# A fused attention and two-layer kernel: block-diagonal q prepared in DRAM, and the padding cleared elsewhere

## The chip, the cores and the metric

The kernel runs on one core of a Trainium2 chip. A core has TensorE (PE) for matrix products, VectorE (DVE) and ScalarE (ACT) for work on elements, GpSimd (POOL), and SyncE (SP), whose queue issues the transfers between DRAM and the on-chip memory. The metric is the device time of one execution in microseconds, median of the runs.

## The reference

Three stages in float32. Attention has 4 batches of 8 heads with 576 positions of 64 numbers; a position sees its own block of 64 positions and all blocks before it. The two layers that follow work on 2304 rows of 512.

```python
scores = scale * np.matmul(q, k.transpose(0, 1, 3, 2))
scores = np.where(block_i >= block_j, scores, -1e9)
attn = np.exp(scores - max);  attn = attn / (sum + 1e-09)
x = (attn @ v).transpose(0, 2, 1, 3).reshape(B * S, H * D)
x = np.maximum(np.maximum(x @ w1, x @ w2), x @ w3) @ w_out      # first layer, d_ff 768
h = x @ w_in;  out = (h * np.cos(h)) @ w_out2                   # second layer, d_ff 2048
```

## The kernel before

**Items.** Attention is cut into 32 items: 4 batches, two halves of the positions (320, then 256), four pairs of heads. The two heads of a pair share the 128 partitions, 64 each. For one block of 64 positions, q of the pair is laid out as a 128x128 block-diagonal tile: head 0 in the upper left quarter, head 1 in the lower right, zeros elsewhere. One product of it with k gives the scores of both heads. An item of the first half has 5 such blocks (640 columns), of the second 4 (512).

**Precision.** From item 4 on, q and k are split into a rounded high part and a rest (`kh`, `kl`; `qbd` holds two tiles, high and low), and the scores take three fast products. The first four items (`NATIVE`, L547) multiply in plain float32 with no split. For them the scale of the scores is applied in the exponential, so that each row maximum (`top`) is multiplied by it first (`scaled`).

**Zeros before.** The layout is made on the chip: tiles are cleared once (`qnat` for the first items, `qbd` by a cast of zeros), and each item then writes the two diagonal quarters, from partitions 0 to 63 and 64 to 127, so there are two loads (first items) or two scalings and two differences (others), the loop over `a` in `load` (L565) and `prep` (L590). The tiles of probabilities (`prob`) are cleared as well, since an odd block leaves its last 64 columns unwritten, which the transposes read.

**An item's path.** `load`, `prep`, `scores` (L606: products into the PSUM tiles SA and SB, row maximum on VectorE, exponential with a sum on ScalarE, reciprocal, scaling of the probabilities), `transposes` (L648, PSUM tile tb, copied to `pt`), `pv` (L660, PSUM tile X). The output of items 0 to 3 goes straight into `xhi` and `xlo`, the first layer's input for the first 320 rows; later outputs go to DRAM (`x`) and come back as chunks of 512 rows (`load_x`, L688).

**Weights.** `convert` (L506) turns a 512 KB tile of weights, which comes as pairs of 32-bit words (`raw`), into float32 and splits it: on ScalarE two scalings (`t`, `add`), on VectorE a shift of `t`, an `or` with the sign, an integer addition (CUSTOM_DVE_ANT_0 in the trace, ISA in the order), then a cast `whi` on either engine and a difference `wlo`. The first layer has 18 tiles w and 6 tiles wout.

**Order.** Every call is recorded first. A planner (`forward`, L292, with `backward` for ranks) lays the operations out over five engines by estimated costs, chooses an engine where `choose` offers several, and the instructions are then issued in that order. A tile with a `tag` and `bufs` has so many copies in rotation: the next user waits until all operations on the copy's last user are done. Products of the first layer and conversions fill the gaps between the items.

Of the kernel before, what the change touches and what calls it, by code (L numbers as in the profile page):

```python
# [8 lines left out]
F32 = mybir.dt.float32  # L9
F32R = mybir.dt.float32r  # L10
# [3 lines left out]
AF = mybir.ActivationFunctionType  # L14
ALU = mybir.AluOpType
# [4 lines left out]
P = 128  # L20
NLOW, NHIGH = 320, 256
# [4 lines left out]
def f32(ap):  # L26
    return ap.bitcast(F32)
# [414 lines left out]

def fused_kernel(tc, qk, v2, w1, w2, w3, wout, w_in2, w_out2, out):
    B, HP, _, S = qk.shape
    S //= 2
    D = P // 2
    NFF = w1.shape[0]
    NFC = w_in2.shape[0]
# [4 lines left out]
    scale = 1.0 / math.sqrt(D)  # L453

    R = Plan(tc)
    const = R.open(name="const", bufs=1)
    cv = R.open(name="cv", bufs=1)
    moe = R.open(name="moe", bufs=1)
    cv_start = R.open(name="cv_start", bufs=1)
# [3 lines left out]
    at = R.open(name="at", bufs=1, side="right")  # L463
    ps_x = R.open(name="ps_x", bufs=1, space=PSUM, side="right")

    qnat = [cv_start.tile([P, 5, P], F32, f"qnat{i}") for i in range(2)]
    for t in qnat:
        R.vector.memset(t, 0.0)
    ident = const.tile([P, P], F32, "ident")
    R.gpsimd.memset(ident, 0.0)  # L470
    R.gpsimd.affine_select(out=ident, in_=ident, compare_op=ALU.not_equal, fill=1.0, base=0, pattern=[[-1, P]],
                           channel_multiplier=1)
    halfpi = const.tile([P, 56], F32, "halfpi")[:, :1]
    R.gpsimd.memset(halfpi, math.pi / 2)
    NROT = 3
    top = [[const.tile([P, 1], F32, f"top{i}_{j}") for j in range(5)] for i in range(NROT)]
    scaled = [[const.tile([P, 1], F32, f"scaled{i}_{j}") for j in range(5)] for i in range(NROT)]
    sums = [const.tile([P, 5], F32, f"sums{i}") for i in range(NROT)]

    whi = [[moe.tile([P, NK, P], F32R, f"whi{j}_{m}") for m in range(3)] for j in range(NFF)]  # L480
# [53 lines left out]
    for u in range(2):  # L534
        f = Half()
# [13 lines left out]
    items = []  # L549
    for b in range(B):  # L550
        for half in range(2):
            for pair in range(HP):
                it = Item()
# [2 lines left out]
                items.append(it)  # L556

    prob = [at.tile([P, (b // 2 + 1) * P], F32, f"prob{b}") for b in range(S // 64)]
    for b in reversed(range(S // 64)):
        R.vector.memset(prob[b], 0.0)  # L560
    qbd = [at.tile([P, 5, P], F32R, f"qbd{i}") for i in range(2)]
    for t in qbd:
        R.copy(t.rearrange("p b n -> p (b n)"), prob[S // 64 - 1])

    def load(it):  # L565
        f, src = it.f, qk[it.b, it.pair]
        it.raw = at.tile([P, S + NHIGH], F32, "qk", tag="qk", bufs=2)
        q0 = S if it.half else 0
        if it.native:
            it.q = qnat[it.n % 2]  # L570
            q0 = NLOW + S if it.half else 0
            for a in (0, 64):
                R.sync.dma_start(it.q[a:a + 64, 0:len(f.blocks), a:a + 64],
                                 src[a:a + 64, q0:q0 + f.n].rearrange("p (b n) -> p b n", n=64))
            it.k = it.raw[:, 0:f.nk]
            if it.n == 0:
                conv_next()
            R.sync.dma_start(it.k, src[:, NLOW:NLOW + f.nk])
            if it.n == 0:
                conv_next()  # L580
        elif it.half:
            R.sync.dma_start(it.raw, src[:, NLOW:])
            it.k, it.q = it.raw[:, 0:S], it.raw[:, S:]
        else:
            R.sync.dma_start(it.raw[:, 0:2 * NLOW], src[:, 0:2 * NLOW])
            it.q, it.k = it.raw[:, 0:NLOW], it.raw[:, NLOW:2 * NLOW]
        it.vr = at.tile([P, 5, 2, 64], F32, "vr", tag="vr", bufs=2)
        R.sync.dma_start(it.vr[:, 0:f.nj].rearrange("p j a d -> p j (a d)"), v2[it.b, it.pair, :, 0:f.nj])

    def prep(it):  # L590
        f = it.f
        if it.native:
            return
        nb, nk = len(f.blocks), f.nk
        kh = it.kh = at.tile([P, S], F32R, "kh", tag="kh")[:, :nk]
        kl = it.kl = at.tile([P, S], F32R, "kl", tag="kl")[:, :nk]
        R.copy(kh, it.k)
        R.sub(kl, it.k, f32(kh))
        for a in (0, 64):
            q = it.q[a:a + 64].rearrange("p (b n) -> p b n", n=64)  # L600
            hi, lo = (t[a:a + 64, 0:nb, a:a + 64] for t in qbd)
            R.scale(hi, q, scale)
            R.vector.scalar_tensor_tensor(lo, q, scale, f32(hi), ALU.mult, ALU.subtract)


    def scores(it):  # L606

        f = it.f
        sm = sums[it.n % NROT]
        nb = len(f.blocks)  # L610
        for banks, parts in f.tiles:
            if banks == 2:
                s = ps_x.tile([P, 2, 512], F32, "SA", tag="SA", bufs=1)
            else:
                s = ps_x.tile([P, 1, 512], F32, "SB" if parts[0][0] % 2 == 0 or it.half else "SA", tag="SB" if banks == 1 else "SA", bufs=1)
            for bank in range(s.dims[0][1] if banks == 2 else 1):
                with R.unit():
                    first = True
                    for b, c0, n, c in parts:
                        ks = slice(bank * n, bank * n + n)  # L620
                        i = b - f.first
                        prods = [(it.q[:, i], it.k[:, ks])] if it.native else [
                            (qbd[0][:, i], it.kh[:, ks]), (qbd[0][:, i], it.kl[:, ks]), (qbd[1][:, i], it.kh[:, ks])]
                        for x, (q, k) in enumerate(prods):
                            R.tensor.matmul(s[:, bank, c0:c0 + n], q, k, start=first, stop=x == len(prods) - 1,
                                            skip_group_check=True)
                            first = False
            for b, c0, n, c in parts:
                i = b - f.first
                part = s[:, :, c0:c0 + n] if c == 2 else s[:, 0, c0:c0 + n]  # L630
                bias = top[it.n % NROT][i]
                R.vector.tensor_reduce(bias, part, axis=AX.XY if c == 2 else AX.X, op=ALU.max, negate=True)
                if it.native:
                    bias = scaled[it.n % NROT][i]
                    R.vector.tensor_scalar(bias, top[it.n % NROT][i], scale, None, ALU.mult)
                p = prob[b][:, 0:n * c]
                if c == 2:
                    p = p.rearrange("p (c n) -> p c n", c=2)
                R.scalar.activation(p, part, AF.Exp, bias=bias, scale=scale if it.native else 1.0,
                                    accum_out=sm[:, i:i + 1])  # L640
        R.vector.tensor_scalar(sm[:, 0:nb], sm[:, 0:nb], 1e-9, None, ALU.add)
        R.vector.reciprocal(sm[:, 0:nb], sm[:, 0:nb])
        for b in f.blocks:
            i = b - f.first
            p = prob[b][:, 0:64 * (b + 1)]
            R.scale_rows(p, p, sm[:, i:i + 1])
# [105 lines left out]
    def conv_w(n, pool, bufs):  # L752
        if n < 3 * NFF:
            j, m = divmod(n, 3)
            convert((w1, w2, w3)[m][j], whi[j][m].rearrange("p k e -> p (k e)"),
                    wlo[j][m].rearrange("p k e -> p (k e)"), pool, bufs)
        else:
            j = n - 3 * NFF
            convert(wout[:, j], vhi[j], vlo[j], pool, bufs)
# [21 lines left out]
    def conv_next():  # L781
        n = converted[0]
        if n < 4 * NFF:
            if n % 3 < 2 and not wk:
                conv_w(n, cv_start, 4)
            else:
                conv_w(n, cv, CVR)
            converted[0] += 1
# [15 lines left out]
        R.tensor.matmul(warm[:, 0:P], ident, ident, start=True, stop=True)  # L804
    for n in range(LA):
        load(items[n])
    for n in range(NI + 1):
        conv = CONV.get(n, (0, 0, 0))
        if n:
            transposes(items[n - 1])  # L810
        for step in range(3):
            if step == 1 and n < NI:
                scores(items[n])
                if n + LA < NI:
                    load(items[n + LA])
            if step == 2 and n:
                it = items[n - 1]
                pv(it)
                if it.n == HP - 1:
                    R.close(cv_start)  # L820
                    wk = R.open(cv_start, name="wk", bufs=1)
                done = S * it.b + (S if it.half else NLOW) if it.pair == HP - 1 else 0
                while begun[0] < len(parts) and sum(parts[begun[0]]) <= done:
                    fill += zip([*range(1, 3 * NFF + 1)] + NK * [4 * NFF], moe1_units(begun[0]))
                    begun[0] += 1
            for _ in range(conv[step]):
                conv_next()
            units((0.3, 0.35, 0.35)[step])
        if n + 1 < NI:
            prep(items[n + 1])  # L830
        if n > 9 and n % 3:
            ahead()
# [166 lines left out]
```

## Time and profile before

| | us |
|---|---|
| median of 3 runs (902.95 to 903.24) | 902.98 |
| the profiled execution, its own time | 905.14 |
| its span | 903.3 |

| engine | busy us | share of the span |
|---|---|---|
| PE | 878.9 | 97% |
| PE's weight loads | 739.9 | 82% |
| DVE | 553.7 | 61% |
| ACT | 464.1 | 51% |
| POOL | 0.7 | 0% |

A busy time counts an instruction from its start to its end. Matmuls overlap, and their ends are modelled, so a busy PE may still be slow. The granted clock of PE is a share of its full speed. The share over the whole span hides that the stages differ: attention and conversions come first, the second layer, which is nearly all matmuls, fills the second half.

### The profile page before, as it was taken

What the parts mean: (1) busy time and instruction counts of PE and PEld (TensorE: products, weight loads), DVE (VectorE), ACT (ScalarE), POOL (GpSimd) and SP (SyncE); (2) the same over time, 40 slices, a digit from 0 to 9 for tenths busy, and PEclk for the clock granted to TensorE, in tenths of its full rate; (3) what the DMA queues carried; (4) which work ended last, traced back from release to release, by engine and by line L of the source; (5) the groups of instructions that cost most, each with busy time, mean ns of one, the idle gap of its engine ahead of it and who ended that gap; (6) DMA issues with size and microseconds to landing.
All of it is one profiled execution on the core that took longest, in us unless ns stands there. A gap on an engine that the chain in (4) does not pass through costs nothing.

```text
span 903.3 us, 12655 instructions
## 1 busy us (share of the span) xinstructions
PE 878.9 (97%) x4716; PEld 739.9 (82%) x4716; DVE 553.7 (61%) x1112; ACT 464.1 (51%) x1012; POOL 0.7 (0%) x7
## 2 busy tenths in 40 slices
PE   5789998999999999999999999999999999999998
PEld 4579997888888888888899888888888888888897
DVE  7899997544784457433294499555555545454554
ACT  6899988567874677544353434332233223322333
POOL 0000000000000000000000000000000000000000
PEclk8799999999999999999999999999999999999999
DMA  7545476412661227300352571020001000100000
GB/s 224 182 165 181 147 220 226 155 50 80 216 220 43 65 88 238 97 21 19 134 169 94 228 267 59 8 86 1 1 25 46 1 1 1 47 0 1 18 30 24
DMA packets 42781, 87.59 MB, mean 97 GB/s; under 512 B 7648, under 2 KB 20960, under 8 KB 42720
## 3 DMA queue, kind: packets, MB, share of 16 engines
q1 hardware_dynamic: 42720, 86.79, 29.0%
q8 instruction: 37, 0.61, 0.3%
q14 instruction: 24, 0.20, 0.1%
HBM read 65.93 MB, written 20.84 MB: 96 GB/s over the span
## 4 chain that ended last, share of the span: by engine, by line
PE 91%; ACT 3%; DVE 3%; DMA 2%; issue 1%; SPq 0%; ACTq 0%; DVEq 0%
PE psm L207 53%; PE po L207 22%; PE X L207 5%; PE tb L207 4%; PE SA L207 4%; PE SB L207 3%; ACT prob L207 2%; DMA qnat<-qk 1%; DVE t L207 1%; DMA x<-xs 1%; DMA t<-x 1%; DVE top L207 1%; SPq L207 0%; ACT add L207 0%; ACT t L207 0%
## 5 line engine op out<-in xcount | busy, mean ns | idle before, releaser
L207 PE MATMUL psm<-yh,w_in 128*128 128x512 f32 (+1 forms) x640 | 193.4, 368 | 0.0
L207 PE MATMUL po<-w_out,gh 128*128 128x512 f32 x576 | 177.8, 390 | 0.0
L207 ACT ACTIVATE th<-th,halfpi 128x512 f32<-128x512 f32 (+1 forms) x80 | 54.6, 682 | 190.7 <-DVE th L207 190.7
L207 PE MATMUL psm<-xhi,whi 128*128 128x512 f32 (+2 forms) x360 | 137.3, 381 | 3.2 <-ACT xhi L207 2.2
L207 PE MATMUL psm<-xlo,whi 128*128 128x512 f32 (+2 forms) x360 | 133.5, 371 | 1.3 <-DVE xlo L207 1.2
L207 PEld LDWEIGHTS psm<-yh,w_in 128*128 128x128 f32 x640 | 117.1, 188 | 20.7
L207 PE MATMUL psm<-xhi,wlo 128*128 128x512 f32 (+2 forms) x360 | 133.3, 370 | 0.0
L207 PEld LDWEIGHTS po<-w_out,gh 128*128 128x128 f32 x576 | 107.1, 188 | 21.4
L207 PE MATMUL psm<-yl,w_in 128*128 128x512 f32 (+1 forms) x320 | 117.7, 368 | 0.0
L207 PE MATMUL po<-w_out,gl 128*128 128x512 f32 x288 | 112.0, 389 | 0.0
L207 DVE TENSOR_SCALAR th<-psm 128x512 int32<-128x512 f32 (+1 forms) x80 | 51.0, 638 | 78.6 <-PE psm L207 78.6
L207 DVE TENSOR_TENSOR th<-psm,th 128x512 f32<-128x512 f32 (+1 forms) x80 | 51.0, 638 | 54.9 <-ACT th L207 54.9
L207 PEld LDWEIGHTS psm<-xhi,whi 128*128 128x128 f32 x360 | 68.1, 189 | 13.5 <-ACT xhi L207 2.7
L207 PEld LDWEIGHTS psm<-xlo,whi 128*128 128x128 f32 x360 | 68.0, 189 | 10.9 <-DVE xlo L207 2.5
L207 PEld LDWEIGHTS psm<-xhi,wlo 128*128 128x128 f32 x360 | 67.8, 188 | 9.9
L207 DVE TENSOR_TENSOR gl<-th,gh 128x512 fp32r<-128x512 f32 (+1 forms) x80 | 51.0, 637 | 39.8 <-ACT gh L207 39.6
L207 DVE TENSOR_TENSOR hm<-psm,hm 128x512 f32<-128x512 f32 (+2 forms) x60 | 38.1, 636 | 60.3 <-PE psm L207 59.8
L207 ACT CAST gh<-th 128x512 fp32r<-128x512 f32 (+1 forms) x78 | 45.0, 577 | 54.9 <-DVE th L207 54.8
L207 PEld LDWEIGHTS psm<-yl,w_in 128*128 128x128 f32 x320 | 60.3, 188 | 10.6
L207 ACT COPY pt<-tb 128x512 f32<-128x512 f32 (+1 forms) x98 | 53.6, 563 | 23.9 <-PE tb L207 23.5
L207 PEld LDWEIGHTS po<-w_out,gl 128*128 128x128 f32 x288 | 54.0, 188 | 11.4
L207 PE MATMUL tb<-ident,prob 128*128 128x128 f32 x400 | 58.6, 276 | 2.5 <-ACT pt L207 1.0
(99 smaller groups left out, 1346.9 us busy)
## 6 DMA issues: line engine op xcount, KB each, us to landing
raw<-w SPq DMA_DIRECT2D x18, 512.0 KB, 4.1
raw<-w_in SPq DMA_DIRECT2D x16, 512.0 KB, 3.8
raw<-w_out SPq DMA_DIRECT2D x16, 512.0 KB, 3.8
qk<-qk SPq DMA_DIRECT2D x16, 416.0 KB, 3.8
vr<-v SPq DMA_DIRECT2D x16, 320.0 KB, 3.9
kept_in<-both SPq DMA_DIRECT2D x10, 512.0 KB, 3.5
w_in<-kept_in SPq DMA_DIRECT2D x10, 512.0 KB, 9.2
out<-osb SPq DMA_DIRECT2D x18, 256.0 KB, 2.0
```

Of the source, the lines that this page charges most:

```text
L207: return lambda: getattr(real, method)(*[value(a) for a in args], **{k: value(a) for k, a in kw.items()})
```

## The change

q is laid out block-diagonal, zeros included, in DRAM by the host's arrangement of the input, so q has twice as many bytes (640 columns an item in the first half, 512 in the second). An item loads it in one transfer into one tile and treats it in one scaling and, from item 4 on, one difference over 128 partitions. The clears of `qnat` and the casts into `qbd` go. k and q now have separate transfers and tiles; for the first items there are two copies of each, for the others one of each, where one tile `qk` in two copies held both. For the first four items k is multiplied by the scale in place before the scores, and `scaled` goes. Of the `prob` tiles only the 64 padding columns of the five that have them are cleared, on GpSimd. The tile that holds `halfpi` is wider and otherwise unchanged.

```diff
-    qnat = [cv_start.tile([P, 5, P], F32, f"qnat{i}") for i in range(2)]
-    for t in qnat:
-        R.vector.memset(t, 0.0)
...
-    for b in reversed(range(S // 64)):
-        R.vector.memset(prob[b], 0.0)
-    qbd = [at.tile([P, 5, P], F32R, f"qbd{i}") for i in range(2)]
-    for t in qbd:
-        R.copy(t.rearrange("p b n -> p (b n)"), prob[S // 64 - 1])
+    for b in range(0, S // 64, 2):
+        R.gpsimd.memset(prob[b][:, 64 * (b + 1):], 0.0)
 
     def load(it):
         f, src = it.f, qk[it.b, it.pair]
-        it.raw = at.tile([P, S + NHIGH], F32, "qk", tag="qk", bufs=2)
...
+        nq = len(f.blocks) * P
         if it.native:
...
+            it.q = cv_start.tile([P, 5 * P], F32, "qnat", tag="qnat", bufs=2)
+            it.k = cv_start.tile([P, NLOW], F32, "knat", tag="knat", bufs=2)
         else:
...
+            it.q = at.tile([P, 5 * P], F32, "q", tag="q")[:, :nq]
+            it.k = at.tile([P, S], F32, "k", tag="k")[:, :f.nk]
+        q0 = 2 * NLOW + S if it.half else 0
+        R.sync.dma_start(it.q, src[:, q0:q0 + nq])
+        R.sync.dma_start(it.k, src[:, 2 * NLOW:2 * NLOW + f.nk])
...
     def prep(it):
         f = it.f
         if it.native:
+            R.scale(it.k, it.k, scale)
             return
...
-        for a in (0, 64):
-            q = it.q[a:a + 64].rearrange("p (b n) -> p b n", n=64)
-            hi, lo = (t[a:a + 64, 0:nb, a:a + 64] for t in qbd)
-            R.scale(hi, q, scale)
-            R.vector.scalar_tensor_tensor(lo, q, scale, f32(hi), ALU.mult, ALU.subtract)
+        it.qh, it.ql = (at.tile([P, 5 * P], F32R, n, tag=n)[:, :len(f.blocks) * P] for n in ("qh", "ql"))
+        R.scale(it.qh, it.q, scale)
+        R.vector.scalar_tensor_tensor(it.ql, it.q, scale, f32(it.qh), ALU.mult, ALU.subtract)
...
-                if it.native:
-                    bias = scaled[it.n % NROT][i]
-                    R.vector.tensor_scalar(bias, top[it.n % NROT][i], scale, None, ALU.mult)
...
+    prep(items[0])
```

The planner orders all engines anew. On SP, the head of the queue before (`qnat_83` is item 0's q, loaded in halves, `raw` a tile of weights, `qk` a k):

```order
L207 DMA qk<-qk 128x320
L207 DMA raw<-w 128x1024
L207 DMA qnat_83<-qk 64x5x64
L207 DMA qnat_91<-qk 64x5x64
L207 DMA raw<-w 128x1024 x3
L207 DMA qk<-qk 128x320
L207 DMA raw<-w 128x1024
L207 DMA qnat_83<-qk 64x5x64
L207 DMA qnat_91<-qk 64x5x64
L207 DMA vr<-v 128x384 x2
```

and now (`knat` and `qnat` are k and q of the first four items; `k` and `q` of 576 and 512 columns are item 4's):

```order
L207 DMA knat<-qk 128x320
L207 DMA qnat<-qk 128x640
L207 DMA knat<-qk 128x320
L207 DMA raw<-w 128x1024
L207 DMA qnat<-qk 128x640
L207 DMA raw<-w 128x1024
L207 DMA k<-qk 128x576
L207 DMA q<-qk 128x512
L207 DMA vr<-v 128x384
L207 DMA raw<-w 128x1024 x2
```

Item 0's q moved from the third and the eighth line to the second, the first weights from the second to the fourth, and item 4's k and q came into the first ten.

On VectorE, the last conversions before the first row maximum of item 0, and what follows, before:

```order
L207 TENSOR_SCALAR t<-t 128x512
L207 ISA t<-t,add 128x1024
L207 SCALAR_TENSOR_TENSOR t<-raw,t 128x512
L207 TENSOR_SCALAR t<-t 128x512
L207 ISA t<-t,add 128x1024
L207 SCALAR_TENSOR_TENSOR t<-raw,t 128x512
L207 TENSOR_TENSOR wlo_1_192<-t,whi_1_183 128x512
L207 ISA t<-t,add 128x1024
L207 TENSOR_REDUCE top_4_210<-SB 128x1
L207 TENSOR_REDUCE top_2_212<-SB 128x1
L207 TENSOR_SCALAR scaled_4_216<-top_4_210 128x1
```

and now, from VectorE's first instruction:

```order
L207 TENSOR_REDUCE top_4_138<-SB 128x1
L207 TENSOR_REDUCE top_2_142<-SB 128x1
L207 TENSOR_REDUCE top_3_149<-SA 128x1
L207 TENSOR_REDUCE top_1_155<-SA 128x1
L207 TENSOR_REDUCE top_0_160<-SA 128x1
L207 TENSOR_SCALAR t<-t 128x512
L207 SCALAR_TENSOR_TENSOR t<-raw,t 128x512
L207 ISA t<-t,add 128x1024
L207 TENSOR_REDUCE top_4_183<-SB 128x1
L207 TENSOR_REDUCE top_2_187<-SB 128x1
L207 TENSOR_SCALAR add<-raw 128x512
```

The clears (eleven, at the head before) and the first four conversions no longer stand ahead of the first maximum, and `scaled` is gone.

On SP again, the loads of the later items, before (`qk` of 832 columns holds k and q of an item of the second half, `vr` is v, `x_0` the output of item 4):

```order
L207 DMA raw<-w 128x1024 x2
L207 DMA vr<-v 128x640
L207 DMA raw<-w 128x1024
L207 DMA vr<-v 128x640
L207 DMA qk<-qk 128x832
L207 DMA raw<-w 128x1024 x3
L207 DMA vr<-v 128x640
L207 DMA x_0_856<-xs 128x256
L207 DMA qk<-qk 128x640
L207 DMA raw<-w 128x1024
```

and now, for the same stretch:

```order
L207 DMA raw<-w 128x1024 x2
L207 DMA vr<-v 128x640
L207 DMA k<-qk 128x576
L207 DMA raw<-w 128x1024
L207 DMA q<-qk 128x512
L207 DMA raw<-w 128x1024 x3
L207 DMA vr<-v 128x640
L207 DMA x_0_784<-xs 128x256
L207 DMA k<-qk 128x576
L207 DMA q<-qk 128x512
L207 DMA raw<-w 128x1024 x3
L207 DMA q<-qk 128x640
```

The k and the q of an item are two lines, with weights between them, and each waits for the item before to have read the one tile there is.

On PE, 8 of the 16 warm-up matmuls on `ident` stand ahead of item 0's scores now, where all 16 did.

## Rows read from the trace of the kernel before

**Rows 1.** Busy time of each engine by stage, granted clock, DMA (columns: first line).
```profile
core 0: us, PE busy (x) PEld busy (x) DVE busy (x) ACT busy (x) POOL busy (x), PEclk, DMA share, GB/s
14.30:18.00 3.70, 3.65 (x10) 2.90 (x10) 1.86 (x7) 2.76 (x7) 0.00 (x0) 0.50 0.65 234
18.00:57.20 39.20, 29.93 (x157) 20.53 (x157) 35.95 (x106) 34.12 (x99) 0.00 (x0) 0.86 0.51 166
57.20:98.50 41.30, 40.86 (x307) 37.90 (x307) 40.61 (x88) 38.37 (x84) 0.00 (x0) 1.00 0.53 172
98.50:139.00 40.50, 40.50 (x318) 37.42 (x319) 38.50 (x100) 36.63 (x103) 0.00 (x0) 1.00 0.63 196
139.00:152.00 13.00, 11.04 (x72) 8.56 (x70) 10.02 (x20) 9.55 (x20) 0.00 (x0) 1.00 0.75 240
517.00:903.30 386.30, 382.71 (x1778) 320.23 (x1776) 221.55 (x368) 122.26 (x202) 0.00 (x0) 1.00 0.11 39
```

**Rows 2.** Start in order of time: start us, us, engine, operation, out<-in, [idle before].
```profile
0.74 0.39 SPq L207 DMA_DIRECT2D qk<-qk  x1
...
1.18 0.42 SPq L207 DMA_DIRECT2D raw<-w  x1
...
1.36 5.53 PE L207 MATMUL psm<-ident 128*128 128x128 f32 x32 [1.36 <-POOL ident L207]
...
2.23 3.37 DVE L207 MEMSET prob<- 128x384 f32 x9
...
4.15 1.35 ACT L207 CAST qbd<-prob 128x640 fp32r<-128x640 f32 x2 [1.92 <-DVE prob L207]
...
5.41 0.67 ACT L207 ACTIVATE t<-raw 128x512 f32<-128x512 f32 x1
...
6.11 0.43 DVE L207 TENSOR_SCALAR t<-t 128x512 int32<-128x512 int32 x1 [0.51 <-ACT t L207]
...
14.31 2.05 PE L207 MATMUL SB<-qk,qnat 128*128 128x320 f32 x4 [7.43 <-DMA qnat<-qk]
...
16.40 0.76 DVE L207 TENSOR_REDUCE top<-SB 128x1 f32<-128x320 f32 x2 [1.18 <-PE SB L207]
...
18.32 1.24 PE L207 MATMUL SB<-qk,qnat 128*128 128x320 f32 x4 [0.36 <-ACT prob L207]
```

**Rows 3.** Chain that ended last, first 20 us: start us, us, what.
```profile
6.27 7.80 DMA qnat<-qk
```

**Rows 4.** Order of time at 55 to 58 us: fourth xlo, and first layer's dense stretch.
```profile
55.15 0.48 DVE L207 TENSOR_TENSOR xlo<-X,xhi 128x320 fp32r<-128x320 f32 x1
...
57.17 0.42 PE L207 MATMUL psm<-xhi,whi 128*128 128x320 f32 x1 [0.49 <-ACT hm L207]
```

**Rows 5.** Groups by shape: count | busy us, mean ns of one | idle before.
```profile
L207 DVE SCALAR_TENSOR_TENSOR t<-raw,t 128x512 int32<-128x512 int32 x56 | 38.1, 686 | 0.4
...
L207 ACT ACTIVATE t<-raw 128x512 f32<-128x512 f32 x51 | 34.2, 670 | 8.3 <-DMA raw<-w 2.2 <-DVE yl L207 2.1 <-DVE w_out L207 2.0
...
L207 DVE CUSTOM_DVE_ANT_0 t<-t,add 128x1024 uint16<-128x1024 uint16 x38 | 26.0, 685 | 2.7 <-ACT add L207 1.6
...
L207 DVE TENSOR_SCALAR t<-t 128x512 int32<-128x512 int32 x56 | 23.4, 421 | 13.0 <-ACT t L207 12.8
...
L207 DVE SCALAR_TENSOR_TENSOR qbd<-qk,qbd 64x256 fp32r<-64x256 f32 x32 | 13.3, 415 | 0.7 <-ACT qbd L207 0.2
...
L207 DVE TENSOR_TENSOR wlo<-t,whi 128x512 fp32r<-128x512 f32 x18 | 12.2, 684 | 0.0
...
L207 ACT ACTIVATE qbd<-qk 64x256 fp32r<-64x256 f32 x20 | 8.3, 415 | 4.5 <-PE SB L207 4.2
...
L207 ACT CAST kh<-qk 128x320 fp32r<-128x320 f32 x11 | 5.0, 450 | 0.0
...
L207 DVE TENSOR_SCALAR scaled<-top 128x1 f32<-128x1 f32 x20 | 2.7, 143 | 0.0
```

**Rows 6.** DMA issues: count, KB each, median us to landing.
```profile
qk<-qk SPq DMA_DIRECT2D x12, 320.0 KB, 2.9
...
qk<-qk SPq DMA_DIRECT2D x4, 160.0 KB, 2.7
```

More of the change, by code (lines that the diff above doesn't have):

```diff
@@ L444, in fused_kernel @@
     B, HP, _, S = qk.shape
-    S //= 2
+    S //= 3
     D = P // 2
@@ L472, in fused_kernel @@
                            channel_multiplier=1)
-    halfpi = const.tile([P, 56], F32, "halfpi")[:, :1]
+    halfpi = const.tile([P, 176], F32, "halfpi")[:, :1]
     R.gpsimd.memset(halfpi, math.pi / 2)
@@ L476, in fused_kernel @@
     top = [[const.tile([P, 1], F32, f"top{i}_{j}") for j in range(5)] for i in range(NROT)]
-    scaled = [[const.tile([P, 1], F32, f"scaled{i}_{j}") for j in range(5)] for i in range(NROT)]
     sums = [const.tile([P, 5], F32, f"sums{i}") for i in range(NROT)]
@@ L558, in fused_kernel @@
     prob = [at.tile([P, (b // 2 + 1) * P], F32, f"prob{b}") for b in range(S // 64)]
-    for b in reversed(range(S // 64)):
-        R.vector.memset(prob[b], 0.0)
-    qbd = [at.tile([P, 5, P], F32R, f"qbd{i}") for i in range(2)]
-    for t in qbd:
-        R.copy(t.rearrange("p b n -> p (b n)"), prob[S // 64 - 1])
+    for b in range(0, S // 64, 2):
+        R.gpsimd.memset(prob[b][:, 64 * (b + 1):], 0.0)
     def load(it):
         f, src = it.f, qk[it.b, it.pair]
-        it.raw = at.tile([P, S + NHIGH], F32, "qk", tag="qk", bufs=2)
-        q0 = S if it.half else 0
+        nq = len(f.blocks) * P
         if it.native:
-            it.q = qnat[it.n % 2]
-            q0 = NLOW + S if it.half else 0
-            for a in (0, 64):
[L573 to L583, printed above, removed]
-        else:
-            R.sync.dma_start(it.raw[:, 0:2 * NLOW], src[:, 0:2 * NLOW])
-            it.q, it.k = it.raw[:, 0:NLOW], it.raw[:, NLOW:2 * NLOW]
+            it.q = cv_start.tile([P, 5 * P], F32, "qnat", tag="qnat", bufs=2)
+            it.k = cv_start.tile([P, NLOW], F32, "knat", tag="knat", bufs=2)
+        else:
+            it.q = at.tile([P, 5 * P], F32, "q", tag="q")[:, :nq]
[3 more added lines that the diff above has]
+        R.sync.dma_start(it.k, src[:, 2 * NLOW:2 * NLOW + f.nk])
+        if it.n == 0:
+            conv_next()
         it.vr = at.tile([P, 5, 2, 64], F32, "vr", tag="vr", bufs=2)
@@ L592, in prep @@
         if it.native:
+            R.scale(it.k, it.k, scale)
             return
[L594 to L599, printed above, removed]
-            q = it.q[a:a + 64].rearrange("p (b n) -> p b n", n=64)
-            hi, lo = (t[a:a + 64, 0:nb, a:a + 64] for t in qbd)
-            R.scale(hi, q, scale)
-            R.vector.scalar_tensor_tensor(lo, q, scale, f32(hi), ALU.mult, ALU.subtract)
+        it.kh, it.kl = (at.tile([P, S], F32R, n, tag=n)[:, :f.nk] for n in ("kh", "kl"))
+        R.copy(it.kh, it.k)
+        R.sub(it.kl, it.k, f32(it.kh))
+        it.qh, it.ql = (at.tile([P, 5 * P], F32R, n, tag=n)[:, :len(f.blocks) * P] for n in ("qh", "ql"))
+        R.scale(it.qh, it.q, scale)
+        R.vector.scalar_tensor_tensor(it.ql, it.q, scale, f32(it.qh), ALU.mult, ALU.subtract)
     def scores(it):
@@ L621, in scores @@
                         i = b - f.first
-                        prods = [(it.q[:, i], it.k[:, ks])] if it.native else [
-                            (qbd[0][:, i], it.kh[:, ks]), (qbd[0][:, i], it.kl[:, ks]), (qbd[1][:, i], it.kh[:, ks])]
+                        qs = slice(i * P, i * P + P)
+                        prods = [(it.q[:, qs], it.k[:, ks])] if it.native else [
+                            (it.qh[:, qs], it.kh[:, ks]), (it.qh[:, qs], it.kl[:, ks]), (it.ql[:, qs], it.kh[:, ks])]
                         for x, (q, k) in enumerate(prods):
@@ L638, in scores @@
                     p = p.rearrange("p (c n) -> p c n", c=2)
-                R.scalar.activation(p, part, AF.Exp, bias=bias, scale=scale if it.native else 1.0,
+                R.scalar.activation(p, part, AF.Exp, bias=bias, scale=1.0,
                                     accum_out=sm[:, i:i + 1])
@@ L980 @@
     v2 = v2.reshape(B, H // 2, 2, (S + D) // P, P, D).transpose(0, 1, 4, 3, 2, 5)
+    heads = qT.reshape(B, H // 2, 2, D, S // D, D)
+    qd = np.zeros((B, H // 2, 2, D, S // D, 2, D), q.dtype)
+    for e in range(2):
+        qd[:, :, e, :, :, e] = heads[:, :, e]
+    qd = qd.reshape(B, H // 2, P, 2 * S)
+    kT = kT.reshape(B, H // 2, P, S)
     arrays = {
-        "qk": np.concatenate([qT[..., :NLOW], kT, qT[..., NLOW:]], axis=3).reshape(B, H // 2, P, 2 * S),
+        "qk": np.concatenate([qd[..., :2 * NLOW], kT, qd[..., 2 * NLOW:]], axis=3),
         "v2": np.ascontiguousarray(v2.reshape(B, H // 2, P, (S + D) // P, 2 * D)),
```

## Prediction

> **What bounds the kernel now.** I read four views in turn: busy time by stage, the start in order of time, the chain that ended last, and groups of instructions by shape.
>
> The stages [rows 1] show three regimes. From 57.2 us PE is busy for 40.86 of 41.30 us, then 40.50 of 40.50, and its last stage (386.3 us, the second layer) has almost nothing idle. Up to 139 us VectorE is full as well (40.61 of 41.30, 38.50 of 40.50) and ScalarE nearly (38.37, 36.63). Before 57.2 us PE has little to do: its busy time there is made of few, slow matmuls at a granted clock of 0.50 and 0.86. From 139 to 152 us PE idles 1.96 us: the fill of the first rows is used up, and attention rows come back late through DRAM. So time is won only where PE starves, in the first 57 us and a little at 145; what the change does after 152 us is worth nothing unless it makes PE wait.
>
> The start [rows 2]: the first score matmul starts at 14.31 us after 7.43 us of idle PE, waiting for the second half of q. The chain [rows 3] says why: that half is issued at 6.27 us, behind five 512 KB weight loads, and takes 7.80 us. Meanwhile VectorE clears 11 tiles, ScalarE casts two of zeros, and both convert weights from 5.41 and 6.11 us on. The fourth item's xlo, which the first layer's groups need whole, ends at 55.63 us, and the dense stretch of PE starts at 57.17 [rows 4].
>
> **Start.** Removed: 11 clears and two casts of zeros. They lie beside the first loads; useful work could not start before the first weights came at 5.41 us, so they count for nothing (without that cover they would cost VectorE 4.6 us and ScalarE 1.35). What moves is the queue: the new order issues k and the whole q of item 0 first, before any weights. k (160 KB) is issued at 0.74 us; such loads take 2.7 us [rows 6], so it lands at 3.4, and the scaling in place, 128x320 on ScalarE, costs 0.45 (the nearest row, a cast of that shape [rows 5]): 3.9. q (320 KB) goes second, where weights went at 1.18 us [rows 2]; at 2.9 us [rows 6] it lands at 4.1. Its upper end: those 512 KB were read at 5.41. Half of the 16 warm-up matmuls stand ahead of the scores: half of 5.53 us from 1.36 [rows 2] ends at 4.1, and `ident` now waits behind three small clears on GpSimd, which the trace lacks: between nothing and 1.1 us, three times the mean clear on VectorE (3.37 us for 9 larger ones [rows 2]); I take 0.4, since they are 64 columns wide. First scores at 4.6 us (4.1 to 5.6), 9.7 earlier. The first row maximum follows 2.09 us behind (16.40 − 14.31): 6.7 us.
>
> **From there to the fourth xlo** took 55.63 − 16.40 = 39.2 us. I count VectorE's rows of that stretch in both orders. Out: 20 rescalings of the maximum at 0.143 = −2.9 us. In: two more shifts (0.421), one more or (0.686), one more add (0.685) and one fewer wlo (0.684): +1.5; five more casts of weights, which ScalarE loses (VectorE's price bounded by the shift, 0.421): +2.1; and small changes in the scaling of probabilities and copies of transposes, bounded by ±1. Sum near zero. On ScalarE two scalings of k (0.9), two more weight scalings (1.3) and one more for the low words (0.7) stand against those five casts (0.45 or more each): between −1 and +1. So about 39 us again: fourth xlo at 45.9, dense PE at about 47.5, a lead of 9.7 us on PE.
>
> **What the lead is worth.** It is borrowed. Before, 11 weight tiles are converted ahead of the fourth xlo, now 8. Three conversions come later, each 0.421 + 0.686 + 0.685 + 0.684 = 2.48 us on VectorE and 2 × 0.670 on ScalarE: 7.4 and 4.0 us, casts aside. They fall into the stretch where both engines are full already [rows 1], and PE's next work, the scores of items 4 to 11 and what hangs on them, comes from these engines. Left of 9.7: 2.3 on VectorE, 5.7 on ScalarE; VectorE decides.
>
> Then the preparation of q: per item two scalings and two differences on 64 partitions become one of each with twice the columns. VectorE: two differences of 64x256 at 0.415 against one of 512 columns, 0.686 by the `or` of the same form: −0.14 us; ScalarE: two scalings at 0.415 against 0.670: −0.16 [rows 5]. Items 5 to 11: −1.0 and −1.1 us. 3.3 us so far. Last, VectorE has 2.98 us and ScalarE 3.45 us idle between 139 and 152 [rows 1], partly for want of PE; a PE that is ahead gives some of it back: 0 to 3, I take 0.8. Together −4.1 us by the time the second chunk of rows enters PE; behind it PE is dense and its work unchanged (same matmuls, same shapes), so that stays to the end.
>
> The extra zeros in q cost DMA, not compute: 160 KB more per item; at 240 GB/s, the highest rate of these stages, 0.7 us of a load, in stages where the engines of the DMA are 53 to 75% busy [rows 1]. Hidden, as long as the loads are early enough (second rival).
>
> The execution profiled has 905.14 us, its span 903.3. The sum is made against it: 905.1 − 4.1 = 901.0; the median of the runs, 902.98, lies 2.2 below: 898.9. I forecast 899.0, its own range 896.5 to 901 (items' stretch 39.2 ± 2, the last term 0 to 3).
>
> **Rivals.**
> *The lead stays whole.* Weight conversions have slack: the new order shifts them because they are not due. If attention alone feeds PE, 9.7 us arrive: 902.98 − 9.7 = 893.3, or up to 896. For it: a group of the first layer needs its own weight tile alone, and eight are there when the dense stretch begins. Against it: VectorE's 98% in the 41 us that follow [rows 1]; what is put off must be fitted in there.
>
> *Loads too late.* Before, the tile that holds q and k of the later items exists twice, so item n+2 loads while n+1 still waits. Now q and k have one tile each: the load of the next item is issued when the preparation of the one before has read it, and SP issues in order, so weight loads that wait for their own buffer stand ahead of it. kh and qh wait on ScalarE, kl and ql on VectorE, and all behind them in those queues. For it: in the new order the k of an item stands behind weight loads, and its q behind one more. Against it: a load of 320 KB takes 2.9 us [rows 6] while items follow each other every 9.8 us (39.2 for four); item 4's loads run ahead, seventh and eighth in the queue. Price: each late microsecond in items 5 to 11 counts seven times; at 0.6 us per item the gain of 4.1 is gone, at 1.5 it is +10.5 − 4.1 = +6.4: 909.
>
> *Nothing arrives.* The first useful step on VectorE is at 6.7 instead of 6.11 us, and both engines are then full to 139. If the item stretch costs 43 us instead of 39, the lead is eaten: 902 to 904.
>
> *The clock.* PE had 0.50 (1.2 GHz) in the 3.7 us behind its long idle, and 0.86 in the sparse stretch that followed [rows 1]; item 0's first scores took 2.05 us at 0.50, item 1's 1.24 [rows 2]. If the sparse stretch, now longer before the first layer, ran at 0.50 throughout, each item pays 0.8 us for either half of its scores: 6.5 us for four, and the gain turns into 902.98 − 4.1 + 6.5 = 905. Against it: there is now no 7.4 us idle ahead of the first scores. The Trainium skill (TensorE: Matmul & The Clock Gate, Part 1) calls the half clock the default state, which only activity releases; by that rule this rival is the one to fear, since fewer warm-up matmuls precede the scores. The trace agrees as far as 0.50 after the idle goes.
>
> **Chances.** Forecast 0.54; lead whole 0.15; nothing arrives or slow clock 0.18; loads late 0.13. The range 893.5 to 904.0 holds the first three but their edges, and leaves out the last. A difference under 0.2% (1.8 us) can't be told from none here. Faster: 0.15, nearly all of the forecast (0.52) and a little of "nothing arrives": 0.69. Same: 0.17. Slower: 0.14.
>
> **What would show it.** First scores at 4.1 to 5.6 us; the first maximum near 6.7; the fourth xlo between 44 and 49; PE dense from about 47.5; VectorE over 96% busy from there to 130; PE's wait for the second chunk longer than the 1.96 us of idle now, since PE is ahead of attention; the last 386.3 us unchanged. I am wrong if the items' stretch is far from 39 us, if ScalarE or VectorE wait for q or k loads, or if PE's lead at 47 us and at 152 us is the same.

## The result and the profile after

The changed kernel takes 895.66 us (median of 6 runs, 893.61 to 898.24), the kernel before 903.2 on the same chip (902.95 to 905.12): 7.5 us less, a ratio of 0.9914 (95% interval 0.9896 to 0.9932). The forecast was 899.0 with a range of 893.5 to 904.0. The direction and the range held, the gain was nearly twice the one worked out.

One caution on sizes. The profiled execution of the changed kernel is the fastest of its six (893.61), that of before one of the slower (905.14). So the two traces stand 11.5 us apart, 4.0 more than the medians: 2.05 on the side of the changed kernel, 1.94 on that of the kernel before. How executions of one order of instructions come to differ is looked at below under the clock, for the changed kernel's order alone. The kernel before has one trace, so its 1.94 us stay open, and every lead that is read from it below may be too large by up to that much.

The stages, cut at the first scores and at the start of the dense stretch, and from there on 11.5 us earlier than in [rows 1]:

```profile
core 0: us, PE busy (x) PEld busy (x) DVE busy (x) ACT busy (x) POOL busy (x), PEclk, DMA share, GB/s
5.20:8.00 2.80, 2.80 (x12) 2.29 (x11) 0.76 (x2) 0.51 (x2) 0.00 (x0) 1.00 0.91 265
8.00:18.00 10.00, 6.86 (x50) 5.28 (x48) 9.42 (x27) 9.44 (x28) 0.00 (x0) 0.99 1.02 384
18.00:45.60 27.60, 21.27 (x126) 15.38 (x126) 26.86 (x69) 26.02 (x74) 0.00 (x0) 0.94 0.51 173
45.60:87.00 41.40, 41.07 (x300) 38.63 (x301) 40.50 (x87) 36.91 (x78) 0.00 (x0) 1.00 0.53 177
87.00:127.50 40.50, 38.74 (x309) 33.95 (x307) 40.03 (x103) 36.84 (x103) 0.00 (x0) 1.00 0.68 223
127.50:140.50 13.00, 13.00 (x93) 11.13 (x89) 11.26 (x22) 10.20 (x24) 0.00 (x0) 1.00 0.79 277
505.50:891.80 386.30, 382.70 (x1778) 320.32 (x1776) 221.33 (x368) 122.56 (x202) 0.00 (x0) 1.00 0.11 39
```

The last stage has the same PE time as before (382.70 against 382.71 of 386.3 us): all that was won in these traces was won before it. The clock of the sparse start is 0.94 to 1.00, where [rows 1] had 0.50 and 0.86.

The start, in order of time (start us, us, engine, operation):

```profile
0.73 0.39 SPq L207 DMA_DIRECT2D knat<-qk  x1
...
1.18 0.42 SPq L207 DMA_DIRECT2D qnat<-qk  x1
...
1.64 3.79 PE L207 MATMUL psm<-ident 128*128 128x128 f32 x16 [1.64 <-POOL ident L207]
...
3.00 0.47 ACT L207 ACTIVATE knat<-knat 128x320 f32<-128x320 f32 x1 [0.99 <-DMA knat<-qk]
...
5.22 1.92 PE L207 MATMUL SB<-knat,qnat 128*128 128x320 f32 x4
...
7.17 0.76 DVE L207 TENSOR_REDUCE top<-SB 128x1 f32<-128x320 f32 x2 [7.17 <-PE SB L207]
```

First scores at 5.22 us instead of 14.31 [rows 2]. They wait for no load, but for the warm-up matmuls, which end at 5.43. VectorE does nothing until 7.17.

The fourth xlo and the start of the dense stretch:

```profile
43.57 0.48 DVE L207 TENSOR_TENSOR xlo<-X,xhi 128x320 fp32r<-128x320 f32 x1
...
45.59 0.41 PE L207 MATMUL psm<-xhi,whi 128*128 128x320 f32 x1 [0.49 <-ACT hm L207]
```

Both are 11.58 us earlier than in [rows 4], and the span ends 11.5 us earlier: in these two traces the lead stayed whole. So the question was why it was not given back, as I had said it would be.

### The profile page after: what moved, and what is told of

Same layout as the page of the kernel before. It is cut to its first block, busy times and chain, and to the rows that moved or that the text cites. A ratio compares the mean times of both kernels' runs of the same rounds, so it can differ in the third digit from the quotient of the medians.

```text
span 891.8 us, 12646 instructions
## 1 busy us (share of the span) xinstructions
PE 874.8 (98%) x4716; PEld 737.9 (83%) x4716; DVE 543.9 (61%) x1065; ACT 452.1 (51%) x974; POOL 1.2 (0%) x12
## 4 chain that ended last, share of the span: by engine, by line
PE 86%; DVE 9%; ACT 2%; issue 2%; DMA 1%; POOL 0%; DVEq 0%; ACTq 0%; POOLq 0%
PE psm L207 52%; PE po L207 22%; PE X L207 4%; PE tb L207 3%; DVE t L207 3%; PE SA L207 3%; PE SB L207 3%; DVE top L207 1%; ACT prob L207 1%; DVE wlo L207 1%; DMA raw<-wout 1%; DVE hm L207 0%; DVE ql L207 0%; DVE whi L207 0%; DVE vlo L207 0%
```

## The experiments

Theory 1: the lead is kept because conversions of weights have slack. Theory 2: VectorE bounds everything up to about 130 us, and the gain is the sum of the work and waiting that it is spared. Theory 3: a good part is the granted clock of the start. Each kernel was run in four to twelve executions, beside the kernel before on the same chip; a ratio is always to that one. The changed kernel was not run again beside them, so a difference from its 895.66 us is taken across sessions, and by the intervals of the ratios it is known to about ±2 us.

### One part at a time: e1_first_items and e2_later_items

```diff
 # e1: the kernel before, with the edits for the first four items; main lines
-    qnat = [cv_start.tile([P, 5, P], F32, f"qnat{i}") for i in range(2)]
...
+            it.q = cv_start.tile([P, 5 * P], F32, "qnat", tag="qnat", bufs=2)
+            it.k = cv_start.tile([P, NLOW], F32, "knat", tag="knat", bufs=2)
+            R.sync.dma_start(it.q, qd[it.b, it.pair][:, 0:5 * P])
...
+            R.scale(it.k, it.k, scale)
 # e2: the kernel before, with the edits for items 4 on; main lines
-    qbd = [at.tile([P, 5, P], F32R, f"qbd{i}") for i in range(2)]
...
+            R.sync.dma_start(it.q, qd[it.b, it.pair][:, q0:q0 + nq])
...
+        R.scale(it.qh, it.q, scale)
+        R.vector.scalar_tensor_tensor(it.ql, it.q, scale, f32(it.qh), ALU.mult, ALU.subtract)
```

> The kernel before with only the part for the first four items: their q whole from a block-diagonal copy in DRAM, two tiles each of k and q, k scaled in place, no qnat clears, no scaled. The probability clears and the two casts into qbd stay, and items 4 on are as before. Theory 1 (the head decides: what starts item 0 earlier is kept to the end): first scores at 5 to 6 us, fourth xlo at 44 to 47, the time 894 to 897.5, all or nearly all of the 7.5 us between 903.2 and 895.7. Theory 2 (less work on VectorE decides, each part has its share): the clears (4.6 us) and casts stay, so half of the gain or less, 899 to 901.

> The kernel before with only the part for items 4 on: q block-diagonal from DRAM, one scaling and one difference, one tile each of q and k, no casts into qbd; the first four items and all clears as before. Theory 1: first scores at 14 us as before, the time 902 to 904.5. Theory 2: the 1.0 us saved on VectorE in items 5 to 11 and the casts arrive, 900 to 902. If the single tiles made loads late, 904.5 or more.

e1: 900.77 us against 903.69, ratio 0.9962 (0.9949 to 0.9974). e2: 899.94, 0.9958 (0.9944 to 0.9971). Theory 1 as I had put it falls: the part that starts item 0 earlier does not carry the gain alone, and the other part carries as much. The two add up: 2.9 + 3.75 = 6.7 us, of the 7.5 of the whole change. Their fourth xlo, e1 and then e2:

```profile
46.38 0.48 DVE L207 TENSOR_TENSOR xlo<-X,xhi 128x320 fp32r<-128x320 f32 x1
```

```profile
51.90 0.49 DVE L207 TENSOR_TENSOR xlo<-X,xhi 128x320 fp32r<-128x320 f32 x1
```

In e1 the lead there is 55.63 − 46.86 = 8.8 us, but its span ends only 4.1 earlier (899.2 against 903.3). That is the borrowing that I forecast: more than half is paid back. In e2 the lead is 3.2 us there and 5.7 at the end (897.6): the later items' part earns 2.5 us behind the fourth xlo. The 3.2 us ahead of it begin before any later item: with the casts of zeros gone and all engines planned anew, e2's first scores start at 12.68 us, not at 14.31 as I had expected. So the two parts are not cleanly a start and a later stretch.

### Is added work paid? e9, e5, e6, e13

The same instruction is issued twice, with the same result and the planned order unchanged, so that nothing else moves. In e9 it is the `or` of conversions 0 to 7, in e5 of 12 to 23, in e13 that of the 14 conversions for the second layer that are made during attention; in e6 it is ScalarE's scaling.

```diff
-        R.vector.scalar_tensor_tensor(i32(t), high, SIGN, i32(t), ALU.bitwise_and, ALU.bitwise_or)
+        o = R.vector.scalar_tensor_tensor(i32(t), high, SIGN, i32(t), ALU.bitwise_and, ALU.bitwise_or)
+        if 12 <= converted[0] < 24:
+            o.calls *= 2
```

> The changed kernel, in which the or of the first eight conversions (those ahead of the fourth xlo) is done twice, in the same planned order: 8 times 0.686 = 5.5 us more on VectorE between 7 and 44 us. Theory 1 (VectorE paces the items up to the fourth xlo, and whatever that is late by stays): +4 to +5.5 us, 899.7 to 901.5. If the start has slack too: under 897.5.

> The changed kernel, in which the or of the last twelve weight conversions of the first layer (those that end between 58 and 114 us) is done twice, with the same result and in the same planned order: 12 times 0.686 = 8.2 us more on VectorE in the stretch where it is 95 to 98% busy. Theory 1 (conversions have slack, the lead of PE is not borrowed): 895.5 to 898. My prediction's step (what is put off must be paid on VectorE in the full stretch): 901 to 904.

> The changed kernel, in which the scaling of the high words is done twice in the same twelve conversions: 12 times 0.67 = 8.0 us more on ScalarE between 58 and 114 us. Theory 1: 895.5 to 898. If ScalarE bounds that stretch: 900 to 904.

> The changed kernel, in which the or of the conversions for the second layer that are made ahead (from 118 us on, in the gaps of attention) is done twice, in the same planned order: about 14 times 0.686 = 9.6 us more on VectorE, some 2.7 of it before the second chunk enters PE. The same work cost +8.1 us in the first layer's last twelve conversions. If slack begins where VectorE is no longer full: +0 to +2.7, 895.5 to 898.5. If every conversion is paid: +8 to +9.6, 904 or more.

| run | work added, us | median, us | against 895.66 |
|---|---|---|---|
| e9 | 5.5 VectorE, 7 to 44 us | 900.57 | +4.9 |
| e5 | 8.2 VectorE, 58 to 114 us | 903.8 | +8.1 |
| e6 | 8.0 ScalarE, 58 to 114 us | 899.7 | +4.0 |
| e13 | 9.6 VectorE, from 118 us on | 896.6 | +0.9 |

By the ratios, each to the kernel before beside it, the four read +4.7, +7.9, +4.2 and +0.8 us. So up to 114 us work on VectorE is paid in full or nearly so, although PE is 96 to 99% busy there in the changed kernel; on ScalarE by about half, which neither theory had. Behind that, the same instruction costs almost nothing: 56 of them became 70 in the trace of e13 (ratio 0.9923, 0.9907 to 0.994, which overlaps the changed kernel's). In e5 the waiting appears on PE:

```profile
57.20:98.50 41.30, 37.92 (x275) 33.96 (x272) 41.02 (x89) 33.06 (x73) 0.00 (x0) 1.00 0.54 170
98.50:139.00 40.50, 36.39 (x259) 30.98 (x258) 37.87 (x92) 32.10 (x91) 0.00 (x0) 0.92 0.59 189
```

PE idles 7.5 of 81.8 us there, where the changed kernel idles 2.1 in the same two windows, and the granted clock of the second is 0.92, where the changed kernel has 1.00. So a part of the 8.1 us may have come by the lower clock; no run separates the two. Nor do the waits of PE name VectorE alone: 2.6 us stand against its `vlo`, 4.0 against ScalarE's `pt` and `prob`. It is the added work that tells the engines apart. PE's busy share hid that VectorE sets the pace: a step that puts a conversion off into this stretch does pay for it, as the prediction said.

### The clears: e3_clears_back

```diff
-    for b in range(0, S // 64, 2):
-        R.gpsimd.memset(prob[b][:, 64 * (b + 1):], 0.0)
+    for _ in range(2):
+        R.vector.memset(prob[S // 64 - 1], 0.0)
+    for b in reversed(range(S // 64)):
+        R.vector.memset(prob[b], 0.0)
```

> The changed kernel with the nine clears of whole probability tiles, and two more for the two of qnat, back on VectorE instead of the five small ones on GpSimd. In the changed kernel VectorE waits until its first maximum at 7.2 us, and eleven clears took 4.6 us. Theory 1: they fit ahead of it, 895 to 896.7. Theory 2 (all work of VectorE in the start counts): +4 us, 899 to 900.5.

894.16 us, ratio 0.9892 (0.9877 to 0.9906): eleven clears on VectorE cost nothing in the new order, since they lie in its idle 7.17 us. Here one warm-up matmul stands ahead of the scores, which now do wait for q:

```profile
4.61 2.04 PE L207 MATMUL SB<-knat,qnat 128*128 128x320 f32 x4 [2.46 <-DMA qnat<-qk]
```

### The clock: e7_long_warm and e10_long_warm

```diff
-    for n in range(16):
+    for n in range(48):
         R.tensor.matmul(warm[:, 0:P], ident, ident, start=True, stop=True)
```

> The kernel before with 48 instead of 16 warm-up matmuls, so that PE has work until the first scores at 14.3 us and the granted clock is 1.00 rather than 0.50 there. Theory 3 (a good part of the gain is the clock of the sparse start): 2 to 5 us faster than before, 898 to 901. Theory 1 (VectorE and the queue order pace the start, PE does not): 902 to 903.5.

> The changed kernel with 48 instead of 16 warm-up matmuls; eight still stand ahead of item 0's scores, the others in the gaps of the first items. The same edit made the kernel before 3.1 us faster. If the changed kernel's sparse start has a share in its spread of 893.6 to 898.2: 892 to 894.5, with a clock of 0.998 in most runs. If its clock is full already (0.95 to 1.00 in the stages before 47 us): 895 to 896.5. If the matmuls stand in the way of scores: 897 or more.

On the kernel before the longer warm-up brings 3.1 us (901.07, ratio 0.9968, 0.9958 to 0.9977). Its stages show the clock of 1.00 and 0.91 where [rows 1] has 0.50 and 0.86. The edit changes more than the clock: the planner spread some of the matmuls among the items, and the first scores start at 13.54 us instead of 14.31, so the 3.1 us are not the clock's alone:

```profile
14.30:18.00 3.70, 3.70 (x32) 3.50 (x30) 3.70 (x15) 2.29 (x8) 0.00 (x0) 1.00 0.65 214
18.00:57.20 39.20, 30.93 (x173) 21.98 (x174) 37.73 (x107) 36.08 (x101) 0.00 (x0) 0.91 0.58 182
```

On the changed kernel it brings 0.9 (894.78, ratio 0.99, 0.9885 to 0.9915), not to be told from nothing. The difference, 2.2 us (1.6 by the ratios), is a rough estimate of what the change gained by leaving no idle 7.4 us ahead of the scores; it is as large as its own uncertainty of about 2 us, so this share of the gain is argued, not shown. The clock also goes with a part of the spread of the runs. e13 issues the same order as the changed kernel up to 118 us; its profiled execution (898.72 us) and that of the changed kernel (893.61) in the same ten microseconds:

```profile
18.00:28.00 10.00, 8.29 (x29) 6.36 (x29) 9.11 (x24) 8.72 (x28) 0.00 (x0) 0.67 0.40 131
```

```profile
18.00:28.00 10.00, 8.42 (x43) 6.26 (x44) 9.26 (x25) 8.97 (x29) 0.00 (x0) 0.84 0.40 133
```

The first line is e13's, the second the changed kernel's: with 0.67 instead of 0.84, 29 matmuls are recorded instead of 43 in nearly the same busy time. The reciprocal of the eleventh item then starts 3.2 us later, before any work that is doubled; here the changed kernel's line comes first:

```profile
114.02 0.19 DVE L207 RECIPROCAL sums<-sums 128x5 f32<-128x5 f32 x1
```

```profile
117.20 0.19 DVE L207 RECIPROCAL sums<-sums 128x5 f32<-128x5 f32 x1
```

The end is 5.1 us later (spans of 896.9 and 891.8), with the doubled work of e13 in the last part of it. The clock is not all of the spread: e12 below has five executions with a mean clock of 1.00, and they lie between 892.5 and 895.46 us.

### Tiles and addresses: e4_two_k and e11_narrow

e4 gives k of the later items two tiles, as the tile before had; to make room, two unused widths are cut. e11 has the second edit alone, in the changed kernel's order of instructions.

```diff
-            it.k = at.tile([P, S], F32, "k", tag="k")[:, :f.nk]
+            it.k = at.tile([P, S], F32, "k", tag="k", bufs=2)[:, :f.nk]
 # and, in e11 this alone:
-EDGE = 24
+EDGE = 1
-    halfpi = const.tile([P, 176], F32, "halfpi")[:, :1]
+    halfpi = const.tile([P, 32], F32, "halfpi")[:, :1]
```

> The changed kernel with two tiles in turn for k of the items from 4 on (halfpi and table are narrower to make room). If single tiles cost something now, this gives it back: 2 us or more faster, under 893.7. If the loads are early enough, as the absence of waits for k and q in the trace says: 895 to 896.7.

> The changed kernel with only the narrower halfpi and table of the run with two tiles of k, in the same order of instructions; all later tiles lie at other addresses. If the addresses made that run slow (its matmuls of 512 columns took 391 to 393 ns in the last stage where the changed kernel has 389): 898 to 901. If the two tiles and the new order that they bring did: 895 to 896.7.

e4: 901.11 us, ratio 0.9969 (0.9958 to 0.9981), 5.4 slower than the changed kernel. e11: 899.27, 0.995 (0.9935 to 0.9966): 3.6 of it come from moving tiles to other addresses. The traces show where: from the first product with `w_in` to the last with `w_out` PE takes 396.9 us in both runs with the narrow widths, e4 and e11, and 393.4 in the traces of the kernel before, the changed kernel and every other run, whatever their order ahead of it. Matmuls of the last stage, 510 to 850 us, in e11 and then in the changed kernel (count | busy us, mean ns):

```profile
L207 PE MATMUL psm<-yh,w_in 128*128 128x512 f32 x480 | 159.1, 392 | 0.0
...
L207 PE MATMUL psm<-yl,w_in 128*128 128x512 f32 x240 | 94.0, 392 | 0.0
```

```profile
L207 PE MATMUL psm<-yh,w_in 128*128 128x512 f32 x480 | 157.4, 389 | 0.0
...
L207 PE MATMUL psm<-yl,w_in 128*128 128x512 f32 x240 | 93.4, 389 | 0.0
```

From the start of one of these 512-column products to the next, `w_out`'s included, it is 226.7 ns in the mean in the changed kernel and 228.9 in e11. Nor do they need another engine at work to be slow: over the intervals in which neither VectorE nor ScalarE runs an instruction, the mean is 226.6 ns (142 of them) and 230.2 (160).

Of e4's 5.4 us, 1.8 are left for the second tile and the order that it brings, with the wrong sign: nothing speaks for single tiles being late. Which of the two widths matters, and which tiles then stand badly to each other, was not tried.

### Both edits together: e12_clears_warm

e3's and e10's edits together.

> The changed kernel with the eleven clears back on VectorE and 48 warm-up matmuls, to see whether the two together beat either: 891.5 to 894 if the clears are hidden as before (894.2) and the clock gains 1 to 2 us; 894 to 896 if the clock is full already.

895.04 us, ratio 0.9902 (0.9885 to 0.9919), with a clock of 1.00 in nearly every run. So the full clock brought nothing more that can be seen. e3, e10 and e12 lie 0.6 to 1.5 us under the changed kernel, and their intervals overlap with its own. All beat the kernel before; none can be called better than the changed one.

## Why the prediction was right, and where its sizes failed

**The range.** The stated range held the result because it was wide enough for a rival. 895.66 us lies outside the forecast's own 896.5 to 901, and inside the 893.3 to 896 of "the lead stays whole". One of the signs of being wrong came as well: PE's lead is 11.58 us at the dense stretch and 11.5 at the end. What was right is the direction, the earlier start, and that VectorE sets the pace; the balance of what the lead is worth was not.

**The start.** First scores were due at 4.6 us (4.1 to 5.6) and came at 5.22, the first maximum at 7.17 instead of 6.7. That half of the warm-up stands ahead of the scores was read right; it started 0.3 later and took 3.79 us, where half of the 5.53 was reckoned. That the clears count for nothing is shown (e3).

**The items' stretch.** 39.2 us were forecast from the first maximum to the fourth xlo; it took 44.05 − 7.17 = 36.9, just under the 39.2 ± 2 allowed. The stretch before and after:

```profile
16.40:55.63 39.23, 30.47 (x157) 20.96 (x156) 35.33 (x105) 33.83 (x97) 0.00 (x0) 0.84 0.49 158
```

```profile
7.17:44.05 36.88, 27.95 (x173) 20.63 (x172) 35.48 (x93) 33.95 (x97) 0.00 (x0) 0.95 0.65 230
```

The count of VectorE's rows summed to near zero, and that was right: it is busy for 35.33 and 35.48 us. What the sum left out is its idle time, 3.90 us before and 1.40 after. Behind the first maximum VectorE waits 3.1 us for products of PE before and 1.0 after, and PE has a granted clock of 0.84 and 0.95. That the higher clock is what shortened these waits is likely, and fits the 2.2 us of e7 and e10, but no run changes the clock alone. I had the clock among the rivals with the opposite sign only.

**What the lead is worth.** This is the term that was mis-sized: of a lead of 9.7 us, 7.4 were to be paid back for three conversions, and only 1.0 for the preparation of q and 0.8 of idle time were set against it. The debt is real (e5: 8.1 us for 8.2; e1 pays back 4.7 of 8.8), but it was more than repaid. Two stretches of equal length, from the fourth xlo on, at about the same place in the program; before, then after:

```profile
55.63:151.00 95.37, 93.01 (x698) 84.46 (x698) 90.07 (x211) 84.60 (x208) 0.00 (x0) 1.00 0.62 197
```

```profile
44.13:139.50 95.37, 92.79 (x688) 83.72 (x690) 92.60 (x213) 84.42 (x204) 0.00 (x0) 1.00 0.63 212
```

VectorE's groups that differ in them, before (count | busy us, mean ns | idle before):

```profile
L207 DVE CUSTOM_DVE_ANT_0 t<-t,add 128x1024 uint16<-128x1024 uint16 x16 | 11.0, 685 | 1.0 <-ACT add L207 0.7
...
L207 DVE SCALAR_TENSOR_TENSOR qbd<-qk,qbd 64x256 fp32r<-64x256 f32 (+1 forms) x18 | 8.0, 445 | 0.3
...
L207 DVE TENSOR_TENSOR wlo<-t,whi 128x512 fp32r<-128x512 f32 x7 | 4.7, 684 | 0.0
...
L207 DVE TENSOR_TENSOR both<-t,both 128x512 fp32r<-128x512 f32 x4 | 2.8, 693 | 1.0 <-ACT both L207 0.9
...
L207 DVE TENSOR_SCALAR qbd<-qk 64x256 fp32r<-64x256 f32 (+1 forms) x6 | 2.1, 345 | 0.0
```

and after:

```profile
L207 DVE CUSTOM_DVE_ANT_0 t<-t,add 128x1024 uint16<-128x1024 uint16 x18 | 12.3, 682 | 0.4 <-ACT add L207 0.3
...
L207 DVE TENSOR_TENSOR wlo<-t,whi 128x512 fp32r<-128x512 f32 x10 | 6.8, 678 | 0.0
L207 DVE SCALAR_TENSOR_TENSOR ql<-q,qh 128x512 fp32r<-128x512 f32 (+1 forms) x9 | 6.7, 741 | 0.0
...
L207 DVE TENSOR_TENSOR both<-t,both 128x512 fp32r<-128x512 f32 x3 | 2.1, 693 | 0.8 <-ACT both L207 0.7
...
L207 DVE TENSOR_SCALAR qh<-q 128x512 fp32r<-128x512 f32 x2 | 0.8, 416 | 0.0
```

Three more wlo are there, as forecast, with two more additions only: one conversion of the second layer (`both`) has moved behind the stretch, where e13 shows that such work is nearly free. (There are 14 `both` in all in either kernel.) All groups of conversions together, casts included, are up by 7.9 us. Against them: the preparation of q is down by 8.0 + 2.1 − 6.7 − 0.8 = 2.6 (1.0 forecast; I had not seen that VectorE also made six of the scalings, and counted 7 items where 9 pass), other work of attention by 1.2, and VectorE's idle time from 5.30 to 2.77, by 2.5 (0.8 forecast). The last 1.6 is a remainder: busy times of groups that overlap a little more. 7.9 = 2.6 + 1.2 + 2.5 + 1.6: the lead passes through whole in these two traces. This is an account of where VectorE's time went, not a test; that the second part saves behind the fourth xlo is shown by e2 (3.2 us there, 5.7 at the end).

**The rivals.** "The lead stays whole" describes the trace, but not for its reason: conversions of the first layer have no slack (e5). "Loads too late" is out: behind 45 us only one wait of 0.4 us in the changed trace names a load of k, none one of q. "Nothing arrives" is out; the clock came out the other way.

**What was to be seen.** The fourth xlo (44 to 49) and VectorE above 96% from 47 to 130 us (40.50 of 41.40, 40.03 of 40.50) came true. PE's wait for the second chunk did not grow: the 1.96 us at 139 [rows 1] are gone, and 1.76 us are idle between 87 and 127.5 instead. The waits of PE between 57 and 139 us (in total, times, longest) are small, and the first names the last difference of a weight, `vlo`, on VectorE:

```profile
PE psm L207 <- DVE vlo L207: 1.0, 1, 1.0
PE psm L207 <- ACT hm L207: 0.4, 1, 0.4
```

So the one wait of note is for a conversion, not for the rows of the second chunk.

**By medians.** Of the 7.5 us the two parts carry 2.9 and 3.75 alone (e1, e2). About 2 of the 7.5 may be the clock, by the rough estimate above; the experiments do not split them between the parts. The wider `halfpi`, which I passed over, earns nothing against before (the products of the second layer take 393.4 us in either), but with `halfpi` and `table` both at their narrowest half of the gain is gone (e11). `halfpi` grew by 120 numbers, 480 bytes a partition, in the same edit in which 15 tiles `scaled` went; it may stand there to keep the later tiles where they were. `halfpi` at its width of before was not tried by itself.

## What to carry to other kernels

A busy PE does not say that PE is the bound: double an idempotent instruction on a suspected engine, in an unchanged order, and see how much of it the end time shows. A lead at the start is worth what the engine that sets the pace saves up to the place where it first has slack; so count all its work to that place, the engine choices of a planner included, and not only the path of the first results. When tiles are added or dropped, look at the matmul time of a stage that the edit does not touch.

## What the runs showed of the hardware

- Moving tiles in the on-chip memory, with every instruction in the same order, made the 512-column matmuls of one group 392 ns instead of 389, the second layer's products 396.9 us instead of 393.4, and the kernel 3.6 us longer. The Trainium skill (SBUF — State Buffer, Who interferes with whom) says that PE never waits on anyone. The trace of e11 does not speak against it: the products are slower, 230.2 ns instead of 226.6 from start to start, also where neither VectorE nor ScalarE works. What slows them is not shown.
- The granted clock differs between executions of the same order of instructions (0.67 and 0.84 in one stretch of 10 us), and the execution with the lower clock was 3.2 us behind at 114 us, where attention feeds a full VectorE.
